# Grouped-query attention with a key and value cache: the last V dealt to the DMA engines in uneven pieces, the split V loads whole

## The chip, the cores and the metric

The kernel runs on one core of one Trainium2 chip. A core has a matrix engine (TensorE, PE in the profile), a vector engine (VectorE, DVE), a scalar engine (ScalarE, ACT), a general engine (GpSimd, POOL) and SyncE (SP), which here only issues loads and the store. Sixteen DMA engines move data between the chip's HBM and the core's on-chip memory (SBUF), which has 128 partitions. A load is one instruction on an issuing engine's queue; its rows are shared out among the DMA engines, and each of them counts the load's semaphore up when its share has landed.

The metric is the device time of one execution in microseconds (us), lower is better.

## The reference

There are 8 sequences of 4 new tokens, 32 query heads, 8 key and value heads, 2048 cached keys and values of 128 numbers per head, all in bf16:

```python
q = (x @ wq) as [B, Hq, Sq, Dh]            # 8, 32, 4, 128
k = repeat(k_cache, 4 times over heads)     # cache: [8, 8, 2048, 128]
v = repeat(v_cache, 4 times over heads)
p = softmax(q @ k^T * Dh ** -0.5)           # over the 2048 keys
out = (p @ v as [B, Sq, Hq * Dh]) @ wo      # [32, 512]
```

The two caches are 32 MiB each, wq and wo 4 MiB each. Every byte is read once, some 75.5 MB.

## The kernel before

**Units of work.** The 64 pairs of sequence and key head are worked on in eight units of eight pairs. Units 1 to 6 (`single(u)`) each take one sequence with its eight heads; units 0 and 7 take two sequences with four heads each. For each unit the kernel loads one K and one V of 4 MiB: 128 partitions with two "members" (`NB`) of 16 KB each. A partition holds 64 consecutive keys of one pair.

**One unit.** `turn` (L213) transposes K on DVE, a quarter at a time; `scores` (L251) multiplies on PE; `top` and `exps` (L264, L291) give the softmax's exponentials; `weights` (L305, L315) transposes them and spreads them into block-diagonal tiles; `values` (L331) multiplies by V in two halves of 32 matmuls each. Each of these matmuls reads the same key columns of both members of V (`rhs=v[:, :, key, :]`). For the last unit the first half of `values` reads the first half of each partition's columns of V, the second half the rest. `scaled` and `joined` (L343, L351, L353), `by_tokens` (L375) and `to_rows` (L389, L394) normalise and rearrange the result, and `project` (L403) multiplies it by wo. The first half of wo comes in one load, the second half in four pieces of 8, 5, 2 and 1 of its 16 row blocks.

**Order.** The schedule is written out by hand. The loop over `u` puts `scores(u)` ahead of `values(u - 1)` on PE. All loads stand in one list (`loads`): K0, wq, K1, V0, K2, V1 and so on to V7 and wo. `issue` takes them from the list as places come free in a ring of four 4 MiB slots (`ring`, `take`); a load into a slot waits on SP for the last reader of what it overwrites. V7 takes the slot of K6, wo that of V5. All loads but one member of K0 (ACT's queue) go through SP's queue, in the order of the list.

**How a K or V is cut.** `load_kv` (L133) issues one load for a whole K or V, or one for each member (`by_member`), or one for each half of the columns with both members in it (`by_half`). The list `split` names those that come by member: V0 to V4 and K7. V7 comes by halves. V5 and V6 are whole. wo is loaded at L146, wq at L137, x at L163, and the result is stored at L484.

Of the kernel before, what the change touches and what calls it, by code (L numbers as in the profile page):

```python
# [17 lines left out]
def kernel(  # L18
# [23 lines left out]
    NU = B * Hkv // (G * NB)  # L42
# [30 lines left out]
    ring = ring_pool.tile([128, NR, NB, C * Dh], BF16, name="ring")  # L73
# [14 lines left out]
    def single(u):  # L88
        return FIRST < u < LAST

    def half_of(u):
        return NG - 1 if u == LAST else 0
# [8 lines left out]
    def take(key):  # L101
        slot_of[key] = n_loads[0] % NR
        n_loads[0] += 1
        return slot_of[key]

    whole = [(0, 1)]
    by_half = [(0, 0.5), (0.5, 1)]
    by_member = None

    def load_kv(kind, u, parts, engines=(nc.sync,)):  # L110

        slot = take((kind, u))
        cache = k_cache if kind == "k" else v_cache
        n = C * Dh
        if not single(u):
            rows = cache[NS1:, G * half_of(u) : G * half_of(u) + G].rearrange(
                "b g (s c) d -> (g s) b (c d)", c=C
            )
        elif kind == "v":
            rows = cache[u - 1].rearrange("(b g) (s c) d -> (g s) b (c d)", g=G, c=C)  # L120
        else:
            rows = cache[u - 1].rearrange("h (s c) d -> (h s) (c d)", c=NS * C)
        if kind == "k" and single(u):
            pairs = [(ring[:, slot, :, :].rearrange("p b n -> p (b n)"), rows)]
        elif parts is by_member:
            pairs = [(ring[:, slot, b, :], rows[:, b]) for b in range(NB)]
        else:
            pairs = [
                (ring[:, slot, :, int(h0 * n) : int(h1 * n)], rows[:, :, int(h0 * n) : int(h1 * n)])
                for h0, h1 in parts  # L130
            ]
        for i, (to, of) in enumerate(pairs):
            engines[i % len(engines)].dma_start(to, of)  # L133

    def load_wq():
        slot = take("wq")
        nc.sync.dma_start(  # L137
            ring[:, slot, :, :].rearrange("p b n -> p (b n)"), wq.rearrange("(p r) n -> p (r n)", r=R)
        )

    def load_wo():
        slot = take("wo")
        for gg, cuts in ((0, (0, RW)), (1, (0, 8, 13, 15, RW))):
            rows = wo[gg * G * 512 : (gg + 1) * G * 512, :].rearrange("(p r) j -> p (r j)", r=RW)
            for r0, r1 in zip(cuts, cuts[1:]):
                nc.sync.dma_start(ring[:, slot, gg, r0 * D : r1 * D], rows[:, r0 * D : r1 * D])  # L146
# [5 lines left out]
            loads.append(("k", u + 2))  # L152
    loads.append("wo")
    loads.reverse()
    split = [("v", 0), ("v", 1), ("v", 2), ("v", 3), ("v", 4), ("k", NU - 1)]

    def issue(done):

        while loads and n_loads[0] < done + NR:
            what = loads.pop()  # L160
            if what == "k0":
                load_kv("k", 0, by_member, (nc.sync, nc.scalar))
                nc.sync.dma_start(x_sb[:, :], x.flatten_outer_dims())  # L163
            elif what == "wq":
                load_wq()
            elif what == "wo":
                load_wo()
            elif what in split:
                load_kv(*what, by_member)
            else:  # L170
                load_kv(*what, by_half if what == ("v", NU - 1) else whole)

    issue(0)

    make_identity(nc, ident[:])
# [266 lines left out]
    for u in range(NU + 1):  # L442
# [19 lines left out]
        if u >= 1:  # L462
# [7 lines left out]
            if u == NU:  # L470
                joined(u - 1)
        issue(2 + 2 * u)

    o_last = psum_o.tile([128, DH], FP32, tag="o", name="o_last")
# [40 lines left out]
```

## Time and profile before

| | |
|---|---|
| median of three runs | 190.02 us (184.55, 190.02, 190.17) |
| profiled execution | 184.38 us |
| its span, first to last instruction | 182.5 us |
| PE, DVE, ACT, POOL busy | 136.6, 128.7, 70.3, 39.3 us |
| DMA bytes, mean rate over the span | 75.70 MB, 415 GB/s |
| chain that ended last | DMA 42%, DVE 23%, PE 22% of the span |
| one 4 MiB V, issue to landing, median | 29.6 us |
| granted TensorE clock, mean | 0.963 |

The profile is of one execution. Its span runs from the first to the last instruction that the profiler recorded; the execution's own time is 1.88 us longer. In the DMA row, each digit is the mean busy share of the sixteen DMA engines in one fortieth of the span, in tenths. "q1" is the queue row that SP's loads go through, "q8 instruction" carries the program's own instructions from HBM. In the timeline the columns are start, duration, engine, source line, operation and its tiles; square brackets give idle time before it and what ended that.

### The profile page before, as it was taken

The numbers are of one execution on the slowest core, as the hardware profiler recorded it, in microseconds if no ns is written. First come the engines' busy times: TensorE is split into PE (matmuls) and PEld (weight loads), VectorE is DVE, ScalarE is ACT, GpSimd is POOL, SyncE is SP. The second block draws the span as 40 slices with busy tenths as digits, with TensorE's granted clock in tenths as the row PEclk, the third lists the DMA queues.
The fourth block names the chain that finished last, engine by engine and source line by source line (L and its number), as shares of the span: only waits on it lengthen the run. The fifth ranks groups of instructions, "written<-read, shape, count | busy, mean of one in ns | idle before, by whom it ended". The sixth has DMA issues, their size and how long they took to land.

```text
span 182.5 us, 2386 instructions
## 1 busy us (share of the span) xinstructions
PE 136.6 (75%) x924; PEld 83.3 (46%) x924; DVE 128.7 (71%) x161; ACT 70.3 (39%) x91; POOL 39.3 (22%) x110
## 2 busy tenths in 40 slices
PE   0000076940999999998999898989399977899993
PEld 0000022310348635843783485358234852388971
DVE  6518025738994999599689957995399559967340
ACT  2000020019604940990395079109900792063010
POOL 8800006006200700430080035004400220023000
PEclk9999999995589999999999999999969999999999
DMA  6999999999999998999999999999999999999991
GB/s 226 431 485 395 424 460 406 424 445 449 452 384 427 456 461 382 420 460 452 391 417 453 460 402 418 431 478 424 391 435 424 435 427 435 415 426 438 427 385 42
DMA packets 4938, 75.70 MB, mean 415 GB/s; under 512 B 512, under 2 KB 704, under 8 KB 960
## 3 DMA queue, kind: packets, MB, share of 16 engines
q1 hardware_dynamic: 4784, 73.47, 94.3%
q10 hardware_dynamic: 144, 2.10, 2.8%
q8 instruction: 7, 0.11, 0.2%
q14 instruction: 3, 0.02, 0.0%
HBM read 75.53 MB, written 0.03 MB: 414 GB/s over the span
## 4 chain that ended last, share of the span: by engine, by line
DMA 42%; DVE 23%; PE 22%; issue 4%; ACT 3%; POOL 2%; SPq 1%; ACTq 0%; DVEq 0%; POOLq 0%
DMA ring<-in_wo_dram 16%; PE s_ps L251 16%; DMA ring<-in_k_cache_dram 15%; DVE kt L213 14%; DMA ring<-in_wq_dram 12%; DVE stat L264 4%; PE o_ps L331 4%; ACT p_sb L291 3%; PE psq L425 2%; DVE pt L305 2%; DVE stat L322 1%; POOL p_bd L315 1%; POOL q_bd L231 1%; PE s_ps L403 1%; DVE stat L272 0%
## 5 line engine op out<-in xcount | busy, mean ns | idle before, releaser
L251 PE MATMUL s_ps<-kt,q_bd 128*128 128x512 bf16 x256 | 69.5, 409 | 20.0 <-POOL q_bd L231 9.9
L213 DVE STREAM_TRANSPOSE kt<-ring 128x1024 f32<-128x1024 f32 x64 | 73.9, 1210 | 14.2 <-DMA ring<-in_k_cache_dram 11.4
L331 PE MATMUL o_ps<-ring,p_bd 128*128 128x256 bf16 x512 | 57.2, 273 | 0.0
L251 PEld LDWEIGHTS <-q_bd 128*128 128x128 bf16 x256 | 25.3, 102 | 63.0 <-issue 26.6
L331 PEld LDWEIGHTS <-p_bd 128*128 128x128 bf16 x512 | 49.8, 98 | 6.0 <-issue 0.2
L315 ACT COPY p_bd<-pt 32x1024 bf16<-32x1024 bf16 x44 | 45.8, 1041 | 1.5 <-DVE pt L305 1.1
L291 ACT ACTIVATE p_sb<-s_ps,stat 128x1024 bf16<-128x1024 f32 x16 | 17.7, 1110 | 72.2 <-DVE stat L272 72.2
L315 POOL COPY p_bd<-pt 32x1024 bf16<-32x1024 bf16 x16 | 17.0, 1065 | 105.9 <-DVE pt L305 93.2
L264 DVE TENSOR_REDUCE stat<-s_ps 128x1 f32<-128x1024 f32 x16 | 19.3, 1208 | 3.4 <-PE s_ps L251 3.4
L305 DVE STREAM_TRANSPOSE pt<-p_sb 128x512 f32<-128x512 f32 x16 | 11.4, 712 | 14.0 <-ACT p_sb L291 14.0
L231 POOL COPY q_bd<-qT 32x64 bf16<-32x64 bf16 x64 | 13.1, 231 | 20.7 <-DVE qT L436 19.0
L425 PE MATMUL psq<-ring,xT_sb 128*32 128x512 bf16 x32 | 3.6, 630 | 9.1 <-DMA ring<-in_wq_dram 9.1
L416 PE MATMUL xtp<-ident,x_sb 32*128 32x32 bf16 x4 | 0.3, 195 | 13.3 <-DMA x_sb<-in_x_dram 13.3
L436 DVE STREAM_TRANSPOSE qT<-q_sb 128x64 f32<-128x64 f32 x8 | 1.2, 214 | 8.8 <-ACT q_sb L432 8.8
L177 DVE MEMSET p_bd<- 128x2048 uint32 x3 | 5.3, 1765 | 2.0 <-PEq L499 1.2
L322 DVE TENSOR_SCALAR stat<-of_b,stat 128x2 f32<-128x2 f32 x8 | 6.3, 793 | 0.3
L416 PEld LDWEIGHTS <-x_sb 32*128 32x128 bf16 x4 | 0.2, 117 | 13.3 <-DMA x_sb<-in_x_dram 13.3
L425 PEld LDWEIGHTS <-xT_sb 128*32 128x32 bf16 x32 | 1.3, 140 | 10.5 <-issue 10.1
L432 ACT CAST q_sb<-psq 128x512 bf16<-128x512 f32 x2 | 1.2, 586 | 11.8 <-PE psq L425 11.8
L375 PEld LDWEIGHTS <-perm 128*128 128x128 bf16 x56 | 3.8, 97 | 2.0 <-issue 0.5
L419 ACT COPY xT_sb<-xtp 128x128 bf16<-128x128 bf16 x1 | 0.3, 266 | 11.2 <-PE xtp L416 11.2
L343 ACT ACTIVATE o_sb<-o_ps,stat 128x128 bf16<-128x128 f32 x8 | 2.9, 368 | 4.1 <-PE o_ps L331 3.9
(30 smaller groups left out, 46.4 us busy)
## 6 DMA issues: line engine op xcount, KB each, us to landing
ring<-in_k_cache_dram SPq DMA_DIRECT2D x6, 4096.0 KB, 22.7
ring<-in_v_cache_dram SPq DMA_DIRECT2D x12, 2048.0 KB, 23.6
ring<-in_v_cache_dram SPq DMA_DIRECT2D x2, 4096.0 KB, 29.6
ring<-in_k_cache_dram SPq DMA_DIRECT2D x3, 2048.0 KB, 27.2
ring<-in_wq_dram SPq DMA_DIRECT2D x1, 4096.0 KB, 21.0
ring<-in_k_cache_dram ACTq DMA_DIRECT2D x1, 2048.0 KB, 12.4
ring<-in_wo_dram SPq DMA_DIRECT2D x1, 2048.0 KB, 25.9
ring<-in_wo_dram SPq DMA_DIRECT2D x1, 1024.0 KB, 28.2
```

The costliest lines, as they stand in the source:

```text
L177: nc.vector.memset(t[:, :, :, :, :], 0.0)
L213: nc.vector.transpose(out=out, in_=in_)
L231: nc.gpsimd.tensor_copy(out=qb[k * 32 : (k + 1) * 32, m, :, g, b, :].rearrange("w (j e) q -> w j e q", e=2), in_=qT[of * 32 : (of + 1) * 3 ...
L251: nc.tensor.matmul(s_ps[t // 2][:, t % 2, :], lhsT=q_bd[u % 2][:, m, 2 * j + e, :, :, :].rearrange("w g b q -> w (g b q)"), rhs=rhs, start ...
L264: nc.vector.tensor_reduce(out=stats[u][0][:, h : h + 1], in_=s_ps[h][:, :, :].rearrange("q t n -> q (t n)"), axis=AX, op=ALU.max, negate=True,
L291: nc.scalar.activation(out=out, in_=in_, func=EXP, bias=stats[u][1][:, :], scale=scale, accum_out=stats[u][2][:, h : h + 1],)
L305: nc.vector.transpose(out=pt[:, :, :, :].rearrange("s c q e -> s (c q e)").bitcast(FP32), in_=ps[u, h][:, :, :, :].rearrange("q c s e -> q ...
L315: copy(out=pb[rows, :, g, :, :], in_=pt[rows, :, :, :])
L322: nc.vector.tensor_scalar_mul(stats[u][3][:, :], of_b[:, :], stats[u][4][:, :])
L331: nc.tensor.matmul(o_pss[u][:, :, :], lhsT=pbs[u, h][:, i // 2, :, :, i % 2].rearrange("s g q -> s (g q)"), rhs=v[:, :, key_of(u, h, i // ...
L375: nc.tensor.matmul(o_pms[r // 2][:, r % 2, gg, :], lhsT=perm[:, r, w : w + 128], rhs=o_sbs[u][:, b, :], start=(u == 0 and r % 2 == 0 and g ...
L425: nc.tensor.matmul(psq[g * T : (g + 1) * T, :], lhsT=xT_sb[:, r, :], rhs=w[:, (g * NB + gg) * rep * Dh : (g * NB + gg + 1) * rep * Dh], st ...
```

## The change

The V loads of units 0 to 4 are issued whole, one load of 4 MiB instead of two of 2 MiB. V7, until now two loads (first and second half of the columns, both members in each), becomes seven: of the first half, member 0 in pieces of 112, 5, 5, 5 and 1 partitions, then member 1 with all 128 partitions; then the second half with both members as before. The number of loads in the program stays the same, five fewer early and five more at the end.

```diff
     whole = [(0, 1)]
-    by_half = [(0, 0.5), (0.5, 1)]
     by_member = None
+    dealt = "dealt"
...
         elif parts is by_member:
             pairs = [(ring[:, slot, b, :], rows[:, b]) for b in range(NB)]
+        elif parts is dealt:
+            cuts = (0, 112, 117, 122, 127, 128)
+            pairs = [
+                (ring[p0:p1, slot, 0, : n // 2], rows[p0:p1, 0, : n // 2])
+                for p0, p1 in zip(cuts, cuts[1:])
+            ]
+            pairs.append((ring[:, slot, 1, : n // 2], rows[:, 1, : n // 2]))
+            pairs.append((ring[:, slot, :, n // 2 :], rows[:, :, n // 2 :]))
...
-    split = [("v", 0), ("v", 1), ("v", 2), ("v", 3), ("v", 4), ("k", NU - 1)]
+    split = [("k", NU - 1)]
...
-                load_kv(*what, by_half if what == ("v", NU - 1) else whole)
+                load_kv(*what, dealt if what == ("v", NU - 1) else whole)
```

Here `n` is the 8192 numbers of one member in one partition, so a row of a piece is 8 KB.

## The prediction

> **What bounds the kernel now.** I read the page from the top: busy shares, the 40 slices, the DMA queues, then the chain. No engine is over 75% busy, but the DMA row is full from the second slice to the last but one, and one queue carries the bytes.
>
> ```profile
> PE 136.6 (75%) x924; PEld 83.3 (46%) x924; DVE 128.7 (71%) x161; ACT 70.3 (39%) x91; POOL 39.3 (22%) x110
> ...
> DMA  6999999999999998999999999999999999999991
> ...
> q1 hardware_dynamic: 4784, 73.47, 94.3%
> ...
> q8 instruction: 7, 0.11, 0.2%
> ```
>
> So the kernel ends when SP's stream of loads ends, plus a tail. The timeline of the tail shows which load it is:
>
> ```profile
> 177.84 0.27 PE L403 MATMUL s_ps<-ring,oP 128*32 128x256 bf16 x1
> ...
> 178.46 0.27 PE L403 MATMUL s_ps<-ring,oP 128*32 128x256 bf16 x1 [0.34 <-DMA ring<-in_wo_dram]
> ...
> 179.39 0.27 PE L403 MATMUL s_ps<-ring,oP 128*32 128x256 bf16 x1
> ...
> 179.70 0.41 DVE L482 CAST out_sb<-s_ps 32x256 bf16<-32x256 f32 x1 [2.08 <-PE o_last L403]
> ...
> 180.17 0.35 SPq L484 DMA_DIRECT2D out_dram<-out_sb  x1
> ```
>
> PE runs dry for 0.34 us before the third piece of wo's second half, and starts its last row at 179.39, just behind the last piece. The trace's semaphore events say when that piece landed. Each load counts its semaphore up sixteen times, once per DMA engine, and the sixteen times of the last wo piece are two clusters: nine at 177.54 to 178.35 and seven at 179.04 to 179.35. The slowest engine's 179.35 is what the end hangs on; the nine have 0.7 to 1.8 us to spare.
>
> The clusters come from instruction fetches. The seven q8 packets (16 KB, 0.88 to 0.97 us each, at 53.9, 74.8, 93.5, 116.4, 139.7, 163.3 and 175.0 us) each hold up one DMA engine, which never catches up, since every engine always has loads queued and gets the same bytes of each. The late cluster grows with them: five engines late in the first half of the last V, six in its second half, seven at the end.
>
> **The V loads made whole.** A pair of halves took 9.72 to 9.74 us from landing to landing on the earliest engine, V5 and V6, already whole, 9.71 and 9.73. In the packet records a 16 KB packet takes 611 ns in both, 16 per engine; a pair only has one more 4-byte count-up packet, which costs its engine 6 ns. Five of these go: 0.03 us off every engine. No reader starts later: each matmul of `values` (L331) takes both members, so it waited for the second half anyway. On SP five issues of about 0.4 us go, hidden, as SP mostly waits.
>
> **The last V dealt out.** Before: two loads of 8 KB rows, 16 packets per engine each; an 8 KB packet follows the last after 306 ns. After, one quarter (member 0, first half) comes as 112 + 5 + 5 + 5 + 1 rows. How are rows shared out among the engines? The nearest rows: a 128-row load gives every engine 8 packets, and x with 32 rows gives every engine 2. So I take whole rows dealt evenly: 112 rows are 7 per engine, five rows are one each on five engines, the same five each time, since each load begins its deal anew. No row shows a five-row load; the bounds are an even spread over all sixteen (nothing changes) and all fifteen on one engine (a rival below). The single row is either 309 ns on one engine or sixteen shares of 512 B, about 0.03 us each, estimated from the 46 ns of a 1 KB packet.
>
> - Eleven engines: one row less, -0.31, the share of the single row +0.03, two count-ups more +0.01, less 0.03 from above: **-0.30 us**.
> - Five engines: 7 + 3 instead of 8, +0.61, the share +0.03, five count-ups more +0.03, less 0.03: **+0.64 us**.
>
> [...]
>
> So everything hangs on which five. If all are among the nine early ones, these end at 178.35 + 0.64 = 178.99 at most, the late seven at 179.35 - 0.30 = 179.05: the end gains 0.30. If one of the seven late is among the five, it ends at 179.04 to 179.35 plus 0.64, that is 179.68 to 179.99: the end loses 0.33 to 0.64. The trace doesn't number the engines, but packets can be followed, as each starts 3 to 4 ns before its engine's last one ends. Followed back, the engines held up by q8 are, in the order of the fetches, the 10th, 12th, 15th (or 6th), 16th, 13th, 3rd and 2nd to have begun their first packet (sixteen starts spread over 0.32 us). That looks like consecutive engines with a wrap after the last one; the wrapped ones are then among the first five to start. I therefore take the five as the first to start, with two late ones among them, and the middle of the loss: +0.50 us. The weak spots are that starting order need not be numbering, and that engines of equal phase may be swapped.
>
> **What is moved past what.** The page's SP lines:
>
> ```profile
> 129.10 11.21 SPq L133 DMA_DIRECT2D ring<-in_v_cache_dram  x3
> ...
> 148.45 7.75 SPq L146 DMA_DIRECT2D ring<-in_wo_dram  x5
> ```
>
> The last V is now seven loads instead of two: five more issues, about 2 us of SP. The trace shows loads taking eight semaphores in turn, so a load waits for the one eight places ahead to land. After the change the member-1 load of the first half is eight behind the first member of K7 (landed 145.2, before: issued by 139.9), the second half behind K7's second (150.1), wo's first behind V6 (159.8 instead of 148.5), its later pieces behind the first pieces of the last V (some 162 to 163). Behind these waits on SP stands only the rest of wo and the store at the end. The queue does not run dry: V6 lands at 157.9 to 159.8 and the last V keeps the engines busy to 167.7, 8 us after wo's first issue; a load needs about 1 us from issue to its first packet (0.75 to 1.76 at the start). Cost nothing, as the backlog hides it; without it each late issue would cost its delay.
>
> PE: `values` of the last V must wait for six loads instead of one. An extra wait costs between nothing and the 0.07 us that the chain's longest small issue gaps last: at most 0.35 us. It falls at 167, where PE is 0.6 us ahead of wo's end (0.34 idle and the starts behind the last pieces), so I take nothing. The five engines land the first half at 165.3 at the latest, 1.8 us before PE gets there (167.1).
>
> **Sum.** The profiled execution took 184.38 us, 182.5 of span and 1.88 around it. 184.38 + 0.50 = **184.9 us**. The three runs shown are 184.55, 190.02 and 190.17, their median 5.6 above the execution profiled; nothing in the trace shows what adds that. On the median the same +0.50 would give 190.5. I forecast from the profiled one. A change under 2% (3.7 us) is about what a measurement of this kernel can't tell from none, so the forecast is no change.
>
> **Rivals.**
> 1. All five engines are early ones: 184.38 - 0.30 = 184.1. For it: nine of sixteen are early. Against: the starting order above.
> 2. Slower: every small load costs a fixed time in the stream, during which the engines stand. The nearest price is the lone store at the end, 1.5 us from issue to landing:
>
> ```profile
> ring<-in_wo_dram SPq DMA_DIRECT2D x1, 128.0 KB, 28.0
> ...
> out_dram<-out_sb SPq DMA_DIRECT2D x1, 32.0 KB, 1.5
> ```
>
> Four small loads give +6.0: 190.4. It decides from 0.93 us per load on (4 x 0.93 = 3.7). Against it: the 128 KB piece of wo passes in 0.35 us behind its neighbour, and x, 32 KB, takes each engine 0.09 us between two others. [...]
>
> 3. The fifteen rows all go to one engine: 14 rows more, +4.3 us there. It then ends at 181.8 (the earliest) to 183.6 (the latest), which is 186.9 to 188.7.
> 4. The unexplained 5.6 us stays in the kernel's runs or leaves them, whatever the loads do: 190.5, or against the median before a gain of 5 us that the change did not make.
>
> **How the numbers follow.** Likeliest +0.50: 0.48, its own range 184.7 to 185.1. Rival 1: 0.27. Rival 2: 0.05. Rival 3: 0.06, half of it over 2%. Rival 4: 0.14, 0.11 of it read as faster. So faster 0.11, same 0.78, slower 0.11. The range goes from 183.8 (rival 1 with another 0.3 us, should all waits move up with the loads) to 190.6, since two of three runs shown lie at 190 and the change can add up to 0.64 to them.
>
> **What would show it.** The last wo piece's sixteen landings: five engines shifted by +0.94 against the other eleven. Right: one of the five is last, near 179.9. Rival 1: the clusters close to within 0.3 us and end near 179.0. Rival 2: gaps in the DMA row near 160 us. Rival 3: one straggler beyond 181. The issue of wo should move to about 160 with the row staying full. If wo's first packets come late, my reading of the eight semaphores missed something, and that would make the prediction wrong first.

## The result, and the profile after

The changed kernel is slower by 1.5%: the ratio of its time to that of the kernel before is 1.0151, with a 95% interval of 1.0114 to 1.0187, about 2.8 us on 184.6. That is under the 2% mark and clear of noise. Its six runs took 186.94, 187.45, 187.56, 187.64, 192.69 and 204.57 us, median 187.6; the six of the kernel before 184.55 to 190.24, median 189.94. Some executions of nearly every kernel here take some 4 us or more longer than its others; the comparison leaves them out, and the only profiles of the changed kernel (192.69 us), of `m112_16` and of `last64` are of such ones.

In the changed kernel's profile the loads moved 385 GB/s from 24 to 64 us, where those of the kernel before moved 432, and then 430 from 76 to 155 us, ahead of the change in the last V. So I read its page from 76 us on.

```profile
PE 135.9 (71%) x924; PEld 83.3 (44%) x924; DVE 128.8 (68%) x161; ACT 70.2 (37%) x91; POOL 39.2 (21%) x110
...
DMA  6999998999999999999999999999999999999991
GB/s 240 422 443 419 350 426 343 381 388 426 357 371 385 435 438 405 419 467 436 409 419 467 440 400 412 436 460 433 409 436 423 423 433 433 294 265 429 435 394 69
...
q1 hardware_dynamic: 4736, 73.47, 94.7%
...
q8 instruction: 7, 0.11, 0.2%
```

The row to look at is the one below the DMA row. The DMA engines are busy in all slices, as before, but in the 35th and 36th slice (162 to 172 us) they move 294 and 265 GB/s. The same row of the kernel before has no such hole:

```profile
GB/s 226 431 485 395 424 460 406 424 445 449 452 384 427 456 461 382 420 460 452 391 417 453 460 402 418 431 478 424 391 435 424 435 427 435 415 426 438 427 385 42
```

The tail of the changed kernel's timeline is as before, only later, and still ends on wo:

```profile
186.70 0.27 PE L412 MATMUL s_ps<-ring,oP 128*32 128x256 bf16 x1 [0.48 <-DMA ring<-in_wo_dram]
...
188.00 0.41 DVE L491 CAST out_sb<-s_ps 32x256 bf16<-32x256 f32 x1 [2.46 <-PE o_last L412]
188.48 0.35 SPq L493 DMA_DIRECT2D out_dram<-out_sb  x1
```

And SP issues wo at 166.64 where it did at 148.45:

```profile
166.64 6.70 SPq L155 DMA_DIRECT2D ring<-in_wo_dram  x5
```

The packet records say what the hole is. In that stretch nearly all 8 KB packets of the last V take 459 to 780 ns, most between 530 and 630, where those outside it take 309. The 16 KB packets of V6 that fall into it take 673 to 1149 ns instead of 611. Nothing stands still (the DMA row stays at 9); everything is slow.

**My first account**, a guess that this trace doesn't show, as it names no partitions: the pieces of 112 and 5 rows are shared out among the engines otherwise than 128 rows are, so that engines get in each other's way where they write into SBUF ("collision", later "write side"). Rivals: wo's late issue, a fixed cost of each small load, the five engines' extra rows ("imbalance"), the whole V loads, and, within the first, the order in which HBM is read ("read side").

### The profile page after: what moved, and what is told of

Same layout as the page of the kernel before. It is cut to its first block, busy times and chain, and to the rows that moved or that the text cites. A ratio compares the mean times of both kernels' runs of the same rounds, so it can differ in the third digit from the quotient of the medians.

```text
span 190.8 us, 2388 instructions
## 1 busy us (share of the span) xinstructions
PE 135.9 (71%) x924; PEld 83.3 (44%) x924; DVE 128.8 (68%) x161; ACT 70.2 (37%) x91; POOL 39.2 (21%) x110
## 4 chain that ended last, share of the span: by engine, by line
DMA 66%; DVE 13%; PE 12%; issue 2%; POOL 2%; ACT 2%; SPq 1%; ACTq 0%; POOLq 0%; DVEq 0%
DMA ring<-in_k_cache_dram 29%; DMA ring<-in_v_cache_dram 17%; DMA ring<-in_wq_dram 12%; DVE kt L222 10%; PE s_ps L260 9%; DMA ring<-in_wo_dram 8%; PE psq L434 2%; ACT p_sb L300 1%; DVE stat L273 1%; POOL p_bd L324 1%; DVE pt L314 1%; POOL q_bd L240 1%; PE s_ps L412 1%; DVE stat L331 0%; POOL q_bd L237 0%
## 5 line engine op out<-in xcount | busy, mean ns | idle before, releaser
L260 PE MATMUL s_ps<-kt,q_bd 128*128 128x512 bf16 x256 | 68.4, 408 | 24.9 <-POOL q_bd L240 10.6
L412 PE MATMUL s_ps<-ring,oP 128*32 128x256 bf16 x32 | 4.4, 272 | 1.7 <-DMA ring<-in_wo_dram 1.7
L412 PEld LDWEIGHTS <-oP 128*32 128x32 bf16 x64 | 3.3, 96 | 2.8 <-issue 2.3
```

The costliest lines, as they stand in the source:

```text
L260: nc.tensor.matmul(s_ps[t // 2][:, t % 2, :], lhsT=q_bd[u % 2][:, m, 2 * j + e, :, :, :].rearrange("w g b q -> w (g b q)"), rhs=rhs, start ...
L412: nc.tensor.matmul(out_ps[half], lhsT=oP[gg][:, r, :], rhs=w[:, r, half * DH : (half + 1) * DH], start=(gg == 0 and r == 0), stop=(gg == N ...
```

## The experiments

### The two halves of the change apart

`whole_only`, against the kernel before:

```diff
-    split = [("v", 0), ("v", 1), ("v", 2), ("v", 3), ("v", 4), ("k", NU - 1)]
+    split = [("k", NU - 1)]
```

> Only the first half of the change: V0 to V4 whole, V7 by halves as before. All theories of the loss put it into the pieces of V7, so 184.6 us, within 0.3 us of the kernel before (the five saved count-ups are worth 0.03). If the whole V loads are what costs, it stands near 187.5, where the changed kernel is.

Measured: ratio 1.0013 (1.0001 to 1.0024), 184.65 to 184.99 us in the runs compared. The whole loads gain nothing; by the interval they cost up to 0.4 us, and the gain of 0.03 us that I gave them can't be seen.

`deal_only`, against the changed kernel:

```diff
-    split = [("k", NU - 1)]
+    split = [("v", 0), ("v", 1), ("v", 2), ("v", 3), ("v", 4), ("k", NU - 1)]
```

> Only the second half: V7 in 112, 5, 5, 5 and 1 rows, V0 to V4 split as before. If the pieces of V7 cost it all, 187.5 us (2.9 above the kernel before), and 8 KB packets of 450 to 750 ns instead of 309 in the stretch of the pieces. If the whole loads have a part in it, less.

Measured: 187.59 and 187.85 us in the two of its four runs that the comparison keeps (too few for an interval), which is the whole loss. Its profile is of the second of these and stands in for the changed kernel's from here on. By stages (from:to, length, busy time and instructions of PE, PE's weight loads, DVE, ACT and POOL, granted clock, and in the last two columns the busy share of the DMA engines and GB/s), first `deal_only`, then the kernel before:

```profile
149.00:157.00 8.00, 5.60 (x23) 1.92 (x21) 6.78 (x7) 2.66 (x4) 0.00 (x0) 1.00 1.02 436
157.00:167.00 10.00, 8.17 (x69) 6.25 (x68) 8.40 (x11) 4.38 (x6) 2.45 (x2) 1.00 1.00 277
167.00:173.00 6.00, 5.59 (x57) 4.95 (x55) 1.56 (x6) 0.74 (x2) 0.00 (x0) 1.00 1.03 437
```

```profile
149.00:157.00 8.00, 5.45 (x22) 1.84 (x21) 6.90 (x7) 2.46 (x4) 0.00 (x0) 1.00 1.01 434
157.00:165.00 8.00, 7.61 (x63) 5.80 (x63) 6.45 (x9) 3.35 (x5) 1.23 (x1) 1.00 0.99 418
165.00:173.00 8.00, 8.00 (x79) 7.22 (x78) 4.40 (x9) 1.78 (x3) 1.23 (x1) 1.00 1.01 430
```

The DMA share is about 1.00 in all of them; the rate falls to 277 for ten microseconds and is whole again before and after. The landings date the loss. From the second member of K7 to the end of V7's first half the sixteen engines took 14.63 us on average before and 18.12 now, 3.49 more; from there to the last piece of wo 14.91 before and 14.79 now. So all of it arises in the pieces and at their edges, and what comes behind them gives back only 0.1 us.

### As many loads, but each with all 128 rows

`cols5`, against the changed kernel:

```diff
-            cuts = (0, 112, 117, 122, 127, 128)
+            cuts = (0, 3072, 3328, 3584, 3840, 4096)
             pairs = [
-                (ring[p0:p1, slot, 0, : n // 2], rows[p0:p1, 0, : n // 2])
-                for p0, p1 in zip(cuts, cuts[1:])
+                (ring[:, slot, 0, c0:c1], rows[:, 0, c0:c1])
+                for c0, c1 in zip(cuts, cuts[1:])
             ]
```

> The changed kernel with the same quarter of V7 cut into five pieces by columns (6 KB and four times 512 B of each row), every piece with all 128 rows: as many loads, the same turn of semaphores and so the same late issue of wo, but each engine gets 8 rows of every piece. Theory 'collision' (rows shared out otherwise than in a 128-row load make engines write into each other's part of the memory): the loss goes, but for the extra packets, some 0.3 us (four packets of about 30 ns more per row instead of a quarter of one of 309), so 184.6 to 185.2. Theory 'late issue' (wo waits for its semaphores): 187.5 stays. Theory 'fixed cost per small load': 187.5 or more stays.

Measured: ratio 1.0011 (0.9998 to 1.0024), 184.80 to 184.92 us in the runs compared. Its stage of the pieces and its issue of wo:

```profile
157.00:165.00 8.00, 7.54 (x63) 5.68 (x62) 6.44 (x9) 3.34 (x5) 1.22 (x1) 1.00 1.00 407
```

```profile
159.96 3.56 SPq L155 DMA_DIRECT2D ring<-in_wo_dram  x5
```

wo is issued 11.5 us later than before, just as the turn of eight semaphores had it, and the whole kernel is at most 0.24% longer. The 512 B pieces land 0.2 us apart. Late issue and a fixed cost per small load are both out as causes of the 2.8 us: it isn't the number of loads. What is left of the difference between the two kernels is how many rows a piece has.

### The quarter evenly dealt, still not in 128 rows

`m112_16` and `last64`, against the changed kernel:

```diff
-            cuts = (0, 112, 117, 122, 127, 128)
+            cuts = (0, 112, 128)      # in m112_16
+            cuts = (0, 64, 128)       # in last64
```

> The changed kernel with the quarter in two pieces, 112 and 16 rows. By even dealing of whole rows each engine gets 7 + 1, as in a 128-row load, so no engine has more than another. Theory 'imbalance' (the five engines with two rows more): 184.6. Theory 'collision': most of the loss stays, since 14/16 of the quarter is still shared out in sevens; 186.3 to 187.3.

> The changed kernel with its quarter of V7 (8 KB rows) in 64 and 64 rows. No engine gets more rows than another. [...] Theory 'imbalance': 184.6.

Measured: `m112_16` 188.1 us in the one of its four runs that the comparison keeps (so no interval), 3.4 above the kernel before and no better than the changed kernel; `last64` ratio 1.0265 (1.0243 to 1.0287), 4.9 us. In neither has any engine more rows than another, by even dealing (the 112-row piece came as 7 packets on each engine in `deal_only`). Imbalance is out as the cause. The rate in the pieces, `m112_16`, then `last64`:

```profile
162.00:171.00 9.00, 7.62 (x65) 5.83 (x64) 7.34 (x10) 4.13 (x6) 1.92 (x2) 1.00 1.01 246
```

```profile
163.00:172.00 9.00, 7.14 (x62) 5.53 (x61) 7.40 (x10) 4.38 (x6) 2.30 (x2) 1.00 1.00 228
```

`last64` cost twice the 2.5 us that I had estimated, eight packets on each engine at twice their 309 ns. The packets in the pieces took 560 to 700 ns by the median of each microsecond, near those 618, but the loads on both sides suffer too: engines are up to 2 us apart, so while the first are in the pieces the late ones are still in V6 (16 KB packets of 688 to 1305 ns), and while the last are in the pieces the first are in the next load.

The start of the stretch points to the company that an engine has there, not to its own load. In `deal_only` the first engine reaches the 112-row piece at 157.48 us, and the first eleven packets of that piece, up to 158.1, still take 309 ns each, while most engines are in V6. As the others come in, the packets go to 460 and, by 159, to some 600 ns.

### Which side collides

V3 lies in the middle of the stream and is four times as large as the quarter. `v3_64_64` and `v3_32_96` are the kernel before with V3 cut by rows; `v3_cross` is `v3_64_64` with other rows read:

```diff
+    by_rows = [(0, 64), (64, 128)]               # in v3_64_64 and v3_cross
+    by_rows = [(32, 96), (0, 32), (96, 128)]     # in v3_32_96
...
+        elif parts is by_rows:
+            pairs = [(ring[p0:p1, slot, :, :], rows[p0:p1, :, :]) for p0, p1 in by_rows]   # in v3_64_64 and v3_32_96
+            pairs = [(ring[p0:p1, slot, :, :], rows[32:96, :, :]) for p0, p1 in by_rows]   # in v3_cross
...
-    split = [("v", 0), ("v", 1), ("v", 2), ("v", 3), ("v", 4), ("k", NU - 1)]
+    split = [("v", 0), ("v", 1), ("v", 2), ("v", 4), ("k", NU - 1)]
...
-                load_kv(*what, by_half if what == ("v", NU - 1) else whole)
+                load_kv(*what, by_half if what == ("v", NU - 1) else by_rows if what == ("v", 3) else whole)
```

> The kernel before, but V3, in the middle of the stream, comes in two loads of 64 rows (partitions 0 to 63, then 64 to 127) instead of one per member. Sixteen engines with 4 rows each, every engine the same bytes. [...] Theory 'read side' (the rows an engine reads from HBM come in another order): no rule which rows hurt; the same loss in the next kernel. Theory 'load count': two loads as before, 184.6.

> As the kernel before, with V3 in loads of partitions 32 to 95, 0 to 31 and 96 to 127. [...] Theory 'read side': the first load reads 64 rows in shares of four exactly like those of the kernel with 64 and 64 rows, so it is as slow as there, and the time is the same or, with a third load, longer.

> As the kernel with V3 in 64 and 64 rows, but both loads read rows 32 to 95 of V3, the rows that came at 611 ns a packet in the kernel that wrote them to partitions 32 to 95; here they are written to partitions 0 to 63 and 64 to 127. (It leaves out rows 0 to 31 and 96 to 127 of V3, which changes unit 3's output and no instruction count.) Theory 'write side': as slow as with 64 and 64 rows, packets near 1290 ns, 197 us. Theory 'read side': the rows read decide, packets at 611 ns, 184.7.

| | ratio (95%) | us more | 16 KB packets of V3 |
|---|---|---|---|
| V3 to partitions 0-63, 64-127 | 1.0679 (1.0660 to 1.0698) | 12.5 | median 1285 ns (91 to 109 us) |
| V3 to 32-95, then 0-31, 96-127 | 1.0412 (1.0379 to 1.0446) | 7.6 | median 611 ns (90 to 94 us), then 1274 (95 to 105) |
| rows 32-95 read, written to 0-63, 64-127 | 1.0701 (1.0635 to 1.0767) | 12.9 | median 1284 ns (92 to 109 us), 1530 to 1750 in the two us before |

The windows of V3 in the three profiles, in this order (a packet counts whole in the window in which it starts, so a DMA share can come out above 1):

```profile
90.00:110.00 20.00, 12.28 (x74) 6.44 (x71) 16.32 (x21) 11.05 (x16) 5.86 (x13) 0.92 1.04 214
```

```profile
90.00:94.00 4.00, 4.00 (x39) 3.59 (x37) 2.79 (x6) 3.98 (x7) 2.28 (x4) 1.00 1.03 438
95.00:105.00 10.00, 8.72 (x43) 3.49 (x40) 9.99 (x10) 3.29 (x4) 0.54 (x3) 1.00 1.11 229
```

```profile
90.00:110.00 20.00, 13.36 (x76) 7.12 (x74) 15.26 (x20) 9.96 (x14) 4.63 (x11) 0.91 1.03 206
```

214, 438, 229, 206 GB/s: a load of 64 rows runs at full rate into partitions 32 to 95 and at half rate into 0 to 63, and the rows that were fast there are slow when they are written here. The write side decides: the same rows came at 438 GB/s into partitions 32 to 95 and at 206 into 0 to 63 and 64 to 127. Why these partitions differ, no run shows.

`v3_64_64` and `v3_32_96` both cost 2.7 us more than half the rate alone, which I estimate at 9.8 and 4.9 (16 and 8 packets on each engine at another 611 ns). Part of it is the edge again: the first 32 KB packets of the next load, K5, took some 2.5 us instead of 1.2, and by the means of the sixteen landings K5 took 1.0 and 1.1 us longer than in the kernel before, and K4 ahead of V3 0.5 longer in the first of the two. Most of the rest lies in V3 itself, which took 10.7 and 6.0 us longer: its slow packets took somewhat more than twice the 611 ns (1285 and 1274, where twice would be 1222).

### The better order at the end of the stream

`last32_96`, against the changed kernel:

```diff
-            cuts = (0, 112, 117, 122, 127, 128)
+            cuts = ((32, 96), (0, 32), (96, 128))
...
-                for p0, p1 in zip(cuts, cuts[1:])
+                for p0, p1 in cuts
```

> The changed kernel with its quarter of V7 in partitions 32 to 95, 0 to 31 and 96 to 127. [...] Theory 'any load of fewer than 128 rows costs alike': 189.6 or, with one load more, above.

Measured: ratio 1.0164 (1.0092 to 1.0237), 3.0 us: below the 4.9 of `last64`, and above the 1.2 that half of its rows at twice the 309 ns would cost (an estimate, four packets on each engine). The two parts can be told apart in its profile, first the load into partitions 32 to 95, then the two of 32 rows:

```profile
157.70:159.20 1.50, 1.41 (x7) 0.54 (x6) 1.50 (x2) 0.00 (x0) 0.00 (x0) 1.00 1.01 426
159.50:164.50 5.00, 4.39 (x45) 3.85 (x44) 3.48 (x6) 3.24 (x5) 1.11 (x1) 1.00 1.04 205
```

The first fifty 8 KB packets, which start between 157.59 and 159.29 us, all take 309 ns, and no 16 KB packet of V6 is slowed beside them; from then on most take 500 to 780. Which rows go to which partitions counts here as in V3, and no cut by rows came down to the kernel before.

None of these kernels beats the kernel before; a version that does didn't come out of them.

## Why the prediction was wrong

**The step that failed** is the deal of the last V, and in it one term: "an 8 KB packet follows the last after 306 ns". I took that from loads of 128 rows and used it for loads of 112 and 5. In the pieces it is mostly 450 to 780 ns, for all sixteen engines and not only for the five with more rows, and the neighbouring loads are slow with them. The sum of +0.64 and -0.30 us per engine weighed rows and left out the place they are written to; what the runs show in its stead is some 3 us on every engine (the sixteen last landings of wo come at 180.59 to 182.60 in `deal_only`, at 177.54 to 179.35 before). I had even noted that no row of the trace shows a five-row load, and then bounded only how its rows are shared out, not how fast they go.

The rivals lacked it as well. Two were on the slower side. The fixed cost per small load gave 190.4, and `cols5` put it at nothing. All fifteen rows on one engine gave 186.9 to 188.7, and the measured time lies inside that by luck alone: in `deal_only` the rows are on five engines, and fourteen of the sixteen last landings come after 181, where that rival had one straggler. The time, 187.6 by the median and about 187.4 by the four runs compared, fell into the stated range only because that range had been stretched for other reasons.

Point by point:

- **What bounds the kernel**: right. The end moved with the last landing of wo, 179.35 to 182.60 in `deal_only`, and the span with it (182.5 to 185.9).
- **Whole V loads at nothing**: right within 0.4 us; the sign of the 0.03 is not shown, and the interval of `whole_only` (1.0001 to 1.0024) lies on the other side of it.
- **How rows are shared**: right as far as the packets show. In `deal_only` each engine's chain has 7 packets of the 112-row piece, and five chains have three more; the single row goes to one engine as a whole. A five-row load counts its semaphore up once at its issue and then five times as it lands, so five engines share it.
- **Which five**: not settled. The +0.50 us took them for the first five engines to start, two late ones among them, and no run shows that a short load goes to the engines that start first. In `deal_only` all five were in the early cluster when V6 came, none of the five engines held up by then was among them, and where the sixth and seventh fetch fell I couldn't follow through the pieces. If all five stayed early, this was rival 1 by the sum as I made it, a gain of 0.3; the runs show some 3 us lost on every engine instead.
- **Late issue of wo**: right, 159.96 in `cols5` and 161.31 in `deal_only` for the 159.8 forecast, hidden by the backlog. In `deal_only` the chain that ended last runs through the issue of wo's second piece at 165.55, but the engines are in the last V until 170.8 at the earliest, so that issue isn't what the end waits for.
- **The early engines' spare time**: misread. Against 179.35 the nine have 1.0 to 1.8 us to spare; 0.7 is the gap between the clusters. The sum doesn't use it.
- **PE waits for six loads**: cost nothing visible. The bound for it was misread, though: the chain has small issue gaps of 0.13 and 0.14 us, so five waits could have cost 0.7 us and not 0.35. The forecast landing of the first half at 165.3 came to 168.02, which used up the 1.8 us of slack. Already V6 came later, and PE, which had gone straight on at 159.90, now stood for it; in the end it still waits for wo:

```profile
161.39 10.64 PE L340 MATMUL o_ps<-ring,p_bd 128*128 128x256 bf16 x96 [1.37 <-DMA ring<-in_v_cache_dram]
...
181.70 0.27 PE L412 MATMUL s_ps<-ring,oP 128*32 128x256 bf16 x1 [0.49 <-DMA ring<-in_wo_dram]
```

**What stays open.** How the loss splits between the 112-row piece and those of five. That the write side decides is shown for loads of 64 and 32 rows (16 KB packets of 1285 and 1274 ns against 611); for the pieces of 112 and 5 it is carried over from these, since their packets slow down too (8 KB packets of mostly 450 to 780 ns against 309). Which engine writes which partitions: the trace names none. And whether any deal could gain: the four cuts of the quarter by rows that were run lost 2.8 to 4.9 us.

## What to carry to other kernels

A load's price per byte didn't carry over here to another cut of the same bytes: 16 KB packets of V3 took 611 ns into partitions 32 to 95 and 1285 into 0 to 63 and 64 to 127. In a stream bound by DMA as this one is, cut by columns and keep the 128 partitions: the quarter of V7 cost some 0.2 us more in five pieces by columns, 2.8 to 4.9 in pieces by rows. Read the GB/s row under the DMA row: in `deal_only` the DMA engines are busy for a share of 1.00 at 277 GB/s, in the kernel before for 1.01 at 434. Where a change makes a kind of load that the trace doesn't show, bound its speed, not only its share of the work.

## What the runs showed that I had not expected

- The slow loads of V3 do a little worse than half the rate: 16 KB packets of 1280 to 1294 ns for the most part, against 611 in the load into partitions 32 to 95.
- Five pieces by columns, four of them 512 B a row, cost some 0.2 us by the runs compared (184.8 to 184.9; the interval, 0.9998 to 1.0024, includes no cost at all), in a stream that is full.
